# A DeltaNet and Fourier-mixing kernel: unread TensorE products between the steps at the first mixing, and three key pieces moved into the next stage

## The chip, the cores and the metric

The kernel runs on one core of a Trainium2 chip. The metric is the device time of one execution in microseconds (us). All ratios in this document are the mean time of one kernel's fast runs over the mean of the other's fast runs of the same rounds, so they are not quite the ratio of the medians that are quoted. The interval behind a ratio is the 95% interval.

## The reference, cut to what matters

The first half is a delta-rule recurrence over 768 positions for 4 batches and 8 heads of 48 columns; the second half mixes the result with a two-dimensional Fourier transform, normalises it and sends it through a two-layer MLP.

```python
for t in range(S):                       # S = 768, B = 4, H = 8, D = 48
    kt, vt, bt = (k_n[:, :, t], v[:, :, t], beta[:, :, t, None])
    y[:, :, t] = np.einsum('bhd,bhde->bhe', q[:, :, t], state)
    v_old = np.einsum('bhde,bhd->bhe', state, kt)
    state = state + bt[..., None] * np.einsum('bhd,bhe->bhde', kt, vt - v_old)
# ... y becomes x of shape (4, 768, 384)
mixed = np.real(np.fft.fft(np.fft.fft(x, axis=1), axis=2)).astype(np.float32)
u = x + mixed
un = (u - mean(u)) / np.sqrt(var(u) + 1e-06)          # over the 384 columns
return u + np.maximum(un @ w_ch1, 0.0) @ w_ch2        # 384 -> 1536 -> 384
```

## The kernel before

The recurrence is cut into chunks of 64 positions: 12 steps for each batch, 48 in all. A step multiplies a state by prepared keys, subtracts (`U`), multiplies by an inverted triangle (`wt`), and updates the state.

```python
def chain(m):
    b, n = divmod(m, NCH)                                   # NCH = 12 steps for a batch
    # ... 8 products of keys and state into pk
    dve.tensor_tensor(U..., V4[:, c]..., pk, op=ALU.subtract)
    yield
    # ... 8 products of wt and U into pu
    act.activation(U..., pu, ACT.Copy)
    yield
    # ...
    if n < NCH - 1:
        # ... 8 products of keys and U into pS
        dve.tensor_tensor(nst, st, pS, op=ALU.add)          # the state update
    # ...
    yield
```

Keys are prepared for eight steps at a time, in "pieces": two kinds of piece transpose keys through PSUM (`pt`) and copy them (`KQT`); the third multiplies them with themselves (`pg`), and four ScalarE copies put the result into the table `A`. The inversion of the group then starts with a VectorE transpose of `A` into `X`; its result is merged into `Z` and `wt`, which step 16, the first of the third group, needs.

```python
def ps_one(shape, name):                                    # pt, pf, pb, pd, ptr, ph, po
    return ps.tile(shape, F32, tag="one", bufs=2, name=name)
# ...
next_keys = keys(4, 5)                                      # twelve pieces, the third group
key_work = {(7, 0): 2, (8, 2): 3, (9, 0): 1, (10, 2): 2, (11, 0): 1, (11, 1): 2, (11, 2): 1}
first_mixing = fourier(0)
for m in range(1, NCH):
    for i, _ in enumerate(chain(m)):
        # ... other work of the step
        advance(next_keys, key_work.get((m, i), 0))
        # ...
run(rest, *later)
later.clear()
advance(first_mixing)
# ...
def ahead(g):
    if g == 2:
        yield from kept(queries(4, 5))                      # kept: held in program order
    # ...
    yield from invert(g)
    for _ in merge(g):
        yield
```

Step 12 (`n == 0`) is the first of the second batch. In its second part (`i == 1`) the loop issues the whole first mixing at once, with the first MLP products beside it, and only after that does it draw from `pre`, which is `ahead(2)`:

```python
pre, due, started = ahead(2), [0.0, 0.0], False
for m in range(NCH, STEPS):
    b, n = divmod(m, NCH)
    # ...
    for i, _ in enumerate(chain(m)):
        if i < 2:
            advancing(later)
        if n == 0 and i == 1:
            run(*later)
            later.clear()
            if b == 1:
                while advance(first_mixing):
                    if (0, 0) in norms or started:
                        started = advance(channels, 2)      # MLP products
            # ...
        if m > NCH or i > 0:
            due[0] += 4.6 if g == 1 else PRE
            due[1] += SIDE[b]
        while max(due) >= 1.0:
            # ... beside() for due[1]
            if due[0] >= 1.0:
                due[0] -= 1.0
                advance(pre)
```

## Time and profile before

| | before |
|---|---|
| time, median of 3 (range) | 775.79 us (775.71 to 776.6) |
| span of the profiled run, mean clock | 773.7 us, 0.971 |
| TensorE (PE) busy, idle | 679.0 us, 94.7 us |
| VectorE (DVE) busy | 391.7 us |
| MLP products `ph` and `po` | 210.1 and 208.5 us of the PE time |

The engine table, the slices, the stretches of the stage and its chain of waits stand in the prediction below. Two views are added here that the prediction did not use, and that would have mattered. The first is the timeline of TensorE in the kernel before; a line is start, length, engine, source line, operation, output<-inputs, their forms, and the number of records.

```profile
143.28 0.68 PE L131 MATMUL pc<-st,KQT 48*64 48x48 f32 x16
...
167.07 0.45 PE L131 MATMUL pc<-st,KQT 48*64 48x48 f32 x16
...
199.50 0.38 PE L131 MATMUL pt<-pack,qp 128*128 128x128 f32 x2
```

The same 16 records of a step took 0.68 us at 143 us and 0.45 us at 167 us, where the clock is recorded as full. So TensorE ran at a low clock at 143 us too, although the clock record shows 1.00 there: it holds no entry before 144.7 us. It had done so from the start: the 192 records of this product before 144.7 us took 303 ns each in the median, those after 195 us 218 ns. What looks like a first drop of the clock at 148 us is therefore one window at full clock, from 144.7 to 148.1 us, in a low clock that lasts from the start of the kernel to 161.8 us. The mean clock of 0.971 counts the time before 144.7 us as full; counted by the length of the products, this profile has 190.0 us at the low clock. And the first work of `ahead(2)`, the query pieces (`pt` from `qp`), ran at 199.5 us, behind the mixing and not in the idle gap at 152 us.

The second is the timeline of VectorE in the kernel before, same columns; the bracket is an idle time before the instruction and what ended it.

```profile
152.00 1.89 DVE L131 STREAM_TRANSPOSE X<-A 128x1024 f32<-128x1024 f32 x1
...
162.82 0.35 DVE L131 TENSOR_TENSOR st<-st,pc 128x192 f32<-128x192 f32 x1 [2.88 <-PE pc L131]
...
224.03 1.98 DVE L131 STREAM_TRANSPOSE Z<-Y 128x1024 f32<-128x1024 f32 x1
...
238.99 0.35 DVE L131 TENSOR_TENSOR U<-V,pc 128x192 f32<-128x192 f32 x1 [8.20 <-PE pc L131]
```

The third group's inversion begins at 152.00 us as soon as `A` is whole, although the program calls it after the query pieces, and it reaches the merge (`Z`) at 224.03 us. VectorE does much other work in between. The last line is the subtraction of step 16.

### The profile page before, as it was taken

The page shows a single profiled execution, that of the slowest core. Times are in us where ns is not written, and L with a number is a line of the kernel's source. Part 1 is how long each engine was busy: PE and PEld are TensorE (multiplying, and loading weights), DVE is VectorE, ACT ScalarE, POOL GpSimd, SP SyncE. Part 2 cuts the span into 40 slices and gives each one's busy share as a digit, 9 for nine tenths or more (in the row PEclk, how much of TensorE's full clock was granted, in tenths as well). Part 3 has the DMA queues.
Part 4 walks back from the last instruction along what each step waited for, and adds up shares of the span by engine and source line. Part 5 has one row for each costly group of instructions (what it writes and reads, how often), then busy time and mean ns, then how long its engine had stood idle before and what let it go on. Part 6 is the DMA issues. An engine that isn't in the chain of part 4 may idle for free.

```text
span 773.7 us, 18281 instructions
## 1 busy us (share of the span) xinstructions
PE 679.0 (88%) x7768; PEld 487.8 (63%) x7768; DVE 391.7 (51%) x972; ACT 261.4 (34%) x708; POOL 83.3 (11%) x116
## 2 busy tenths in 40 slices
PE   5934598779989989899998999899999989899996
PEld 4622477567647757466756667566667667577683
DVE  2599776877980299336597122989311125300000
ACT  3742355643336512533413535112622022121120
POOL 8010033323100000001100000101000000100000
PEclk9999999877999999999999999899999989999999
DMA  8642032342210221001211110100000000000000
GB/s 182 165 108 50 6 86 63 86 121 68 45 39 18 51 44 32 13 22 38 37 27 25 23 38 7 22 11 22 12 22 2 19 4 1 21 1 21 10 11 20
DMA packets 81041, 30.78 MB, mean 40 GB/s; under 512 B 75856, under 2 KB 77392, under 8 KB 80960
## 3 DMA queue, kind: packets, MB, share of 16 engines
q1 hardware_dynamic: 76560, 21.92, 13.3%
q0 software_dynamic: 2224, 7.31, 2.9%
q8 instruction: 61, 1.00, 0.5%
q10 hardware_dynamic: 2176, 0.39, 0.3%
q14 instruction: 20, 0.16, 0.1%
HBM read 24.87 MB, written 4.72 MB: 38 GB/s over the span
## 4 chain that ended last, share of the span: by engine, by line
PE 54%; DVE 14%; ACT 4%; issue 2%; DMA 1%; SPq 1%; POOL 1%; POOLq 0%; DVEq 0%; ACTq 0%
PE ph L131 20%; PE po L131 18%; DVE X L131 4%; PE pc L131 3%; DVE A L131 3%; PE pf L131 2%; PE pb L131 2%; DVE x L131 2%; ACT wt L131 2%; PE pg L131 2%; PE pt L131 2%; PE py L131 2%; ACT A L131 1%; PE ptr L131 1%; PE pj L131 1%
## 5 line engine op out<-in xcount | busy, mean ns | idle before, releaser
L131 PE MATMUL ph<-unT,w 128*128 128x256 f32 x864 | 210.1, 392 | 4.3 <-ACT hT L131 2.7
L131 PE MATMUL po<-w,hT 128*128 128x384 f32 x576 | 208.5, 504 | 0.1
L131 PEld LDWEIGHTS ph<-unT,w 128*128 128x128 f32 x864 | 159.5, 192 | 31.7 <-ACT hT L131 5.9
L131 PEld LDWEIGHTS po<-w,hT 128*128 128x128 f32 x576 | 105.0, 193 | 63.1 <-issue 3.6
L131 ACT ACTIVATE hT<-ph 128x256 f32<-128x256 f32 x144 | 55.1, 383 | 188.8 <-PE ph L131 188.4
L131 DVE TENSOR_TENSOR x<-x,po 128x384 f32<-128x384 f32 x24 | 13.2, 550 | 108.6 <-PE po L131 108.5
L131 PE MATMUL pg<-KQT 48*64 48x64 f32 (+1 forms) x1152 | 44.9, 295 | 9.5 <-ACT KQT L131 7.2
L131 PEld LDWEIGHTS pg<-KQT 48*64 48x64 f32 x1152 | 34.2, 176 | 25.6 <-ACT KQT L131 14.0
L770 POOL DMA_INDIRECT out_dram<-x,rows_hi x12 | 12.4, 1032 | 332.8 <-DVE x L131 174.1
L131 DVE TENSOR_TENSOR U<-V,pc 128x192 f32<-128x192 f32 x48 | 16.7, 348 | 56.8 <-PE pc L131 56.8
L131 ACT ACTIVATE KQT<-pt 128x256 f32<-128x256 f32 (+1 forms) x84 | 33.2, 414 | 30.8 <-PE pt L131 29.7
L131 DVE TENSOR_TENSOR A<-X 128x30 f32<-128x30 f32 (+14 forms) x120 | 41.3, 344 | 3.0
L131 ACT ACTIVATE U<-pc 128x192 f32<-128x192 f32 x48 | 15.9, 331 | 79.1 <-PE pc L131 75.7
L131 DVE TENSOR_TENSOR X<-X,A 128x30 f32<-128x30 f32 (+14 forms) x120 | 40.7, 339 | 2.8
L131 DVE TENSOR_TENSOR st<-st,pc 128x192 f32<-128x192 f32 x44 | 15.4, 350 | 43.5 <-PE pc L131 36.7
L131 PEld LDWEIGHTS pc<-st,KQT 48*64 48x64 f32 x768 | 19.4, 158 | 26.7 <-DVE st L131 16.5
L131 PE MATMUL pc<-st,KQT 48*64 48x48 f32 x768 | 26.1, 253 | 10.9 <-DVE st L131 10.5
L131 PE MATMUL pt<-pack,qp 128*128 128x128 f32 x96 | 22.5, 331 | 13.9 <-DMA qp<-in_q_dram 13.1
L131 PEld LDWEIGHTS pc<-U,wt 64*64 64x64 f32 x768 | 20.2, 154 | 20.4 <-issue 9.6
L131 PE MATMUL pc<-U,wt 64*64 64x48 f32 x768 | 26.9, 249 | 5.9 <-DVE U L131 4.3
L131 ACT ACTIVATE A<-pj 32x128 f32<-32x128 f32 (+1 forms) x76 | 20.8, 274 | 32.5 <-PE pj L131 31.8
L131 DVE TENSOR_TENSOR x<-x,pb 128x191 f32<-128x191 f32 (+1 forms) x72 | 24.8, 414 | 13.6 <-PE pb L131 13.5
(135 smaller groups left out, 846.5 us busy)
## 6 DMA issues: line engine op xcount, KB each, us to landing
x<-in_moe_w_ch_dram SPq DMA_DIRECT2D x14, 384.0 KB, 3.5
qp<-in_q_dram SPq DMA_DIRECT2D x96, 48.0 KB, 2.4
kp<-in_k_dram SPq DMA_DIRECT2D x80, 48.0 KB, 2.5
V<-in_v_dram SPq DMA_DIRECT2D x56, 48.0 KB, 2.5
w<-in_moe_w_ch_dram POOLq DMA_DIRECT2D x6, 384.0 KB, 7.8
x<-in_moe_w_ch_dram POOLq DMA_DIRECT2D x4, 384.0 KB, 7.9
V<-in_v_dram SPq DMA_DIRECT2D x64, 24.0 KB, 2.1
out_dram<-x SPq DMA_DIRECT2D x8, 192.0 KB, 1.9
```

The costliest lines, as they stand in the source:

```text
L131: ins = getattr(self.engine, name)(*args, **kwargs)
L770: nc.gpsimd.indirect_dma_start(out=out.rearrange("b s m -> (b s) m"), out_offset=bass.IndirectOffsetOnAxis(ap=rows_hi[:, i:i + 1], axis=0) ...
```

## The change

Its intent is to keep the TensorE clock up at the first mixing, where TensorE has gaps. A constant table is multiplied with itself into a buffer that nobody reads, up to three times in each of steps 11 to 14. Beside that, three of the twelve key pieces of the third group leave step 11 and become the first work of `ahead(2)` (two others are issued one place later than before).

```diff
+    def busy(m):
+        if NCH - 1 <= m < NCH + 3:
+            mm(ps_one([128, 384], "idle"), stab[:, 0:128], stab[:, 0:384], True)
 ...
     def chain(m):
 ...
         dve.tensor_tensor(U.rearrange(ue, e=2), V4[:, c].rearrange(ue, e=2), pk, op=ALU.subtract)
+        busy(m)
         yield
 ...
         act.activation(U.rearrange(ue, e=2), pu, ACT.Copy)
+        busy(m)
         yield
 ...
             dve.tensor_tensor(nst, st, pS, op=ALU.add)
+            busy(m)
 ...
-    key_work = {(7, 0): 2, (8, 2): 3, (9, 0): 1, (10, 2): 2, (11, 0): 1, (11, 1): 2, (11, 2): 1}
+    key_work = {(7, 0): 2, (8, 2): 3, (9, 0): 1, (10, 2): 1, (11, 0): 1, (11, 2): 1}
 ...
         if g == 2:
-            yield from kept(queries(4, 5))
+            yield from kept(seq(next_keys, queries(4, 5)))
```

## The prediction

> **What bounds the kernel now.** I read the engine table first, then the slices, then the stage that the diff touches: steps 11 to 14 of the recurrent chain and the first mixing, 143 to 195 us.
>
> ```profile
> PE 679.0 (88%) x7768; PEld 487.8 (63%) x7768; DVE 391.7 (51%) x972; ACT 261.4 (34%) x708; POOL 83.3 (11%) x116
> ...
> PE   5934598779989989899998999899999989899996
> ...
> DVE  2599776877980299336597122989311125300000
> ...
> PEclk9999999877999999999999999899999989999999
> ```
>
> Over the whole span TensorE (PE) is the fullest engine, and after 230 us it is busy 510 of 544 us. The clock row shows a dip in slices 8 to 10 (19.3 us each), and there VectorE (DVE) is as full as PE. So this is a stage of two coupled engines, followed by one bound by PE. The next view gives busy time in stretches of 3.41 us; columns are stretch, length, busy us (instructions) of PE, its weight loads, DVE, ACT, POOL, then the clock.
>
> ```profile
> 144.70:148.11 3.41, 1.40 (x44) 0.97 (x36) 3.41 (x9) 2.69 (x8) 0.65 (x2) 1.00 0.30 68
> 148.11:151.53 3.42, 2.42 (x92) 2.42 (x94) 1.83 (x6) 2.82 (x9) 1.33 (x2) 0.50 0.19 30
> 151.53:154.94 3.41, 1.52 (x32) 0.81 (x31) 3.41 (x5) 0.73 (x2) 0.33 (x1) 0.50 0.24 40
> 154.94:158.35 3.41, 2.27 (x28) 2.10 (x23) 3.41 (x13) 0.00 (x0) 0.46 (x1) 0.50 0.21 36
> 158.35:161.77 3.42, 3.42 (x29) 3.10 (x29) 1.59 (x8) 1.00 (x3) 0.83 (x1) 0.50 0.80 262
> 161.77:165.18 3.41, 3.41 (x45) 3.06 (x43) 1.78 (x4) 3.41 (x9) 0.58 (x1) 1.00 0.22 52
> 165.18:168.59 3.41, 2.80 (x59) 2.06 (x57) 3.21 (x10) 1.91 (x5) 1.35 (x2) 1.00 0.69 224
> 168.59:172.01 3.42, 0.45 (x16) 0.32 (x16) 2.99 (x12) 2.20 (x5) 0.80 (x2) 1.00 0.34 107
> 172.01:175.42 3.41, 2.74 (x23) 2.19 (x24) 2.83 (x8) 0.98 (x2) 1.69 (x2) 0.50 0.00 0
> 175.42:178.83 3.41, 3.41 (x10) 2.45 (x10) 3.31 (x6) 0.00 (x0) 3.08 (x2) 0.50 0.51 143
> 178.83:182.25 3.42, 3.42 (x25) 2.41 (x24) 3.01 (x11) 1.15 (x3) 0.59 (x2) 0.50 0.38 121
> 182.25:185.66 3.41, 3.41 (x24) 2.74 (x24) 3.03 (x9) 1.58 (x5) 1.45 (x2) 1.00 0.00 0
> ```
>
> The clock is half in four stretches from 148.1 (13.7 us) and three from 172.0 (10.2 us), each time after a stretch with little PE work (1.40 and 0.45 us). Elsewhere stretches with 1.98 us (223.2) and 1.81 us (284.7) kept the full clock, one with 1.86 us (329.0) lost it. So I put the limit near 1.8 us of 3.41. Which waits follow? In the chain of waits a line is start, length, work:
>
> ```profile
> 172.52 0.49 DVE un L131
> 173.14 1.51 PE ptr L131 x6
> ...
> 175.05 3.15 PE pb L131 x8
> 178.20 2.86 PE ph L131 x6
> ...
> 191.74 0.79 PE pd L131 x4
> ...
> 192.55 1.21 DVE x L131 x4
> ```
>
> From 173.1 to 192.5 the chain that ends last lies on PE without a break, its first 9.1 us at half clock. Then it goes over to DVE (the inversion of the third group), whose result is merged at 233 us and lets step 16 run. The totals of waits from 140 to 235 us add: DVE for PE 3.2 us at the state update, 2.0 and 1.4 us at the mixing's additions; PE for ACT 2.6 us at the key products `pg`; DVE for ACT 2.0 us.
>
> **What the Trainium skill says.** "TensorE: Matmul & The Clock Gate", section "What's actually happening": the clock is either half or full, decided over a free-running window of about 3.4 us. The trace agrees: every change lies on a grid of 3.41 us, which is why I cut the view so. Its section "Why this matters for your kernels" asks for no idle gap above about 3 us; here PE had been idle 1.6 us (146.5 to 148.1) when the clock fell, so this trace goes by the busy share of the window. "FP8 and Floating Point Precision", section "TensorE Precision Notes", gives true FP32 four passes; an estimate for 384 columns at 2.4 GHz is 4 x 384 / 2.4 = 640 ns. The trace has two records for each such product: 24 records of `po` (128x384) took 8.01 us, 334 ns each, 667 ns a product. It agrees.
>
> **The change, part by part.**
> 1. Dummy products. Step 11 calls it twice (its state update, with the third call, is skipped as the last step of a batch), steps 12 to 14 three times: 11 products, 22 records, 11 x 0.667 = 7.3 us of PE at full clock, 14.7 us at half. They read only the table, so they wait for no data, but each takes one of two PSUM buffers shared with `pf`, `pb`, `pt`, `ph`, `po`.
> 2. Where they lie. PE's idle gaps in the stage are 146.5 to 149.1, 152.8 to 154.7, 155.5 to 156.7, 168.0 to 171.0 and several of about 0.6 us up to 173.1, some 10 us. By their place in the program, the two of step 11, the first of step 12 and two or three of step 13 fall beside these: about 6, free. The other 5 fall into full stretches: 3.3 us of added work, of which I put 2.6 us (the last of step 13, three of step 14) on the chain above.
> 3. What they buy. Window 144.7: 1.40 + 2 x 0.667 = 2.7 us, over the limit, so the first drop should go. In window 151.5 the work at full clock is about 0.8, a dummy makes 1.5, and the three displaced key pieces (two pairs of transposes at about 0.4, one `pg` at 0.7) make 3.0, so it should hold. The mixing's `pf` then runs at full speed: PE is busy about 5.0 us from 156.7 to 161.7, so up to 2.5 us less, and DVE's 2.9 us wait at 159.9 shrinks by as much. Window 168.6 has 0.45, plus one or two dummies: 1.1 to 1.8 us, at the limit. If it holds, 9.1 us at half clock become 4.6, up to 4.5 us less on the chain; even if it fails, step 14's dummies make the next windows denser and may end the slow part a window early (about 1.7 us).
> 4. Key pieces. Three of twelve (two transposes with copies, one `pg` with four ACT copies, 2.1 us of ACT) leave step 11, where ACT is the queue that PE (2.6 us) and DVE (1.6 us of the 2.0) wait for, and go where ACT idles 7.8 us (152.5 to 160.3). Worth about 1 us. Against it, the 1.9 us transpose that starts the inversion comes later; it stood ahead of step 12's state copy, so DVE only swaps the two.
>
> Sum: first drop -2.5, second drop half of -4.5 = -2.2, key pieces -1, dummies on the path +2.6, gives -3.1 us. DVE allows it: it is idle 13 us between 140 and 230, 6.6 of it the three waits for PE above. The dense PE stage after 233 us hands any earlier end of the merge through to the end nearly whole. I add -0.9 us because the later windows of the stage get a shorter wait on `pb` and `pd` (3.4 us), which I have only counted in part.
>
> **Rivals.** *The clock stays low anyway*: window 168.6 remains below the limit, or a displaced dip appears. For it: 1.1 us is a likely value there. Then about -2 to +1: 774 to 777. *The dummies become the wait*: they need a buffer that DVE empties only after six additions (2.1 us), and [...]a dummy stuck for a buffer holds real products. For it: both buffers are in use in the mixing; against it, the real products there wait for the same buffers. Up to +3: 777 to 779. *DVE is the bound*: it is busy 8.9 us of 10 from 170 to 180, so faster PE only makes PE wait; the gain halves, 773 to 774. *Everything holds*: full clock from 144.7 on, -7 us or a little more: 767 to 769.
>
> **Range and chances.** The predicted time is 775.79 - 4.0 = 771.8 us. The good rival and the bad one give 765.5 to 777.5 us. Faster by 2% means under 760.3 us, 15.5 us less, more than the 13 us that DVE idles in the stage: 0.02. Slower by 2% needs twice the whole 7.3 us of dummies: 0.01. Within 2%: 0.97.
>
> **What would show it.** In the changed kernel the clock at 148 to 162 us should read 1.00, and at 172 to 182 us shorter or gone; 22 records of `idle` of about 0.33 us spacing; the wait at the state update (2.9 us) below 1 us; `pd` ending 2 to 5 us before 192.5; step 16's first products 3 to 5 us before 238. The prediction is wrong if the clock dips remain in number and length, if `idle` shows waits for DVE or ACT above 1 us each, or if the gain at 230 us is lost again to a clock drop later on.

## The result and the profile after

The changed kernel took 783.67 us in the median of 4 runs (783.06 to 787.03), the kernel before 776.19 us (775.71 to 776.72, 4 runs): a ratio of 1.0105 (1.0075 to 1.0135). Run again later with five rounds the ratio was 1.0077 (1.0041 to 1.0113). It is within 2%, as most of the chances said, but it is slower by 6 to 8 us and lies outside the range of 765.5 to 777.5 us.

The engine table and three of the rows of 40 slices (19.5 us each) of the kernel after:

```profile
PE 689.3 (88%) x7790; PEld 489.8 (63%) x7790; DVE 391.6 (50%) x972; ACT 260.5 (33%) x708; POOL 84.1 (11%) x116
...
PE   5934588979987999899998999899999989899996
...
DVE  2599776856785169746597111988411125300000
...
PEclk9999999989999999999999999899999999999999
```

TensorE has 22 more records, the 11 unread products, and is busy 10.3 us more. Its idle time fell by only 2.6 us (94.7 to 781.4 - 689.3 = 92.1 us); the difference is the 7.7 us of the longer span. VectorE does the same work (391.6 us), but is less full in the slices 9 to 11, counted from 1 (5, 6, 7 tenths; before 7, 7, 9), and does more of it later. The clock row dips less, but the record of this kernel begins only at 155.8 us, and the products before that are as slow as in the kernel before (`pc` from `st`: 303 ns). Counted from the start the low clock lasts 190.9 us here and 190.0 us before.

The next view is the stretches of 3.41 us of the kernel after, with the prediction's columns (stretch, length, busy us of PE, its weight loads, DVE, ACT, POOL, the clock, and two DMA columns).

```profile
155.79:159.20 3.41, 3.41 (x57) 3.15 (x57) 2.83 (x11) 0.79 (x2) 1.52 (x1) 1.00 0.35 62
159.20:162.62 3.42, 3.42 (x44) 2.96 (x42) 0.35 (x1) 2.27 (x7) 0.10 (x1) 1.00 0.92 317
...
166.03:169.44 3.41, 0.79 (x40) 0.54 (x32) 3.39 (x12) 1.09 (x3) 0.58 (x2) 1.00 0.60 205
169.44:172.86 3.42, 2.29 (x17) 1.77 (x17) 2.51 (x7) 1.91 (x5) 2.03 (x3) 0.50 0.02 5
...
179.68:183.10 3.42, 3.42 (x18) 3.03 (x17) 2.44 (x8) 2.83 (x8) 1.79 (x3) 1.00 0.20 31
```

In this profile the low clock ends at 155.79 us instead of 161.77 us, so the mixing's first products run at full clock. The second dip stays, from 169.44 to 179.68 us (10.2 us, as before), after a stretch with 0.79 us of TensorE work. Where were the unread products that should have filled it? They are `idle` in the timeline of TensorE of the kernel after:

```profile
143.97 1.65 PE L131 MATMUL idle<-stab 128*128 128x384 f32 x2
...
152.53 3.35 PE L131 MATMUL idle<-stab 128*128 128x384 f32 x4
...
196.48 0.38 PE L131 MATMUL pt<-pack,kp 128*128 128x128 f32 x2
...
198.73 0.81 PE L131 MATMUL idle<-stab 128*128 128x384 f32 x2
```

Two records are one product. Four products ran by 155.9 us (a line at 147.38 us is left out), at 1.65 us each where a product at full clock takes 0.81 us; none ran between 155.9 and 198.7 us; the other seven came from 198.7 to 217.9 us, where TensorE is full anyway. The moved key pieces (`pt` from `kp`, then `pg`) came at 196.5 us.

VectorE's timeline after shows what those pieces hold up:

```profile
160.13 0.35 DVE L131 TENSOR_TENSOR st<-st,pc 128x192 f32<-128x192 f32 x1 [1.51 <-PE pc L131]
...
200.08 1.97 DVE L131 STREAM_TRANSPOSE X<-A 128x1024 f32<-128x1024 f32 x1 [7.99 <-ACT A L131]
...
238.11 2.03 DVE L131 STREAM_TRANSPOSE Z<-Y 128x1024 f32<-128x1024 f32 x1
```

The state update waits 1.51 instead of 2.88 us: the gain that was looked for. It did not come a second time. In a later profile of the same kernel (h1 below) the low clock lasted to 163.8 us, the first block of the mixing (`pf`, 14 records) took 2.94 us as before, not 1.62 us, and the same update waited longer than before:

```profile
163.09 0.35 DVE L131 TENSOR_TENSOR st<-st,pc 128x192 f32<-128x192 f32 x1 [4.75 <-PE pc L131]
```

So two profiles of one kernel disagree on whether the early products shorten the low clock. Over all 18 profiles it is not shown that they do: from 140 to 165 us the nine with early products have 10.9 to 23.8 us of low clock, the nine without 15.9 to 24.1 us. In the first profile, the inversion starts at 200.08 instead of 152.00 us, after 7.99 us in which VectorE stood idle until `A` was whole, and `Z` is made 14.1 us later. From 160 to 200 us VectorE idled some 19 us, before 9 us. The subtraction of step 16 moved from 238.99 to 250.98 us. The chain of waits of the kernel after tells it in one piece:

```profile
189.97 6.67 PE ph L131 x30
...
197.22 0.37 PE pt L131 x2
197.83 0.74 PE pg L131 x29
198.59 0.67 ACT A L131 x2
...
200.08 1.98 DVE X L131
```

Five groups of MLP products (`ph`), then the key pieces, then ScalarE's copies to `A`, then the inversion. Where are the 7.7 us lost? Every kernel leaves 1440 records of MLP products (`ph` and `po`) on TensorE, so the end of the n-th of them tells how far the work that must be done has come. The 48th ended 3.0 us earlier than before, the 96th 2.6 us later (218.5 us before), the 144th 1.7 us later (237.3), the 288th 5.9 us later (303.9), the last 7.7 us later. So 5.6 us go between records 48 and 96, where the late key pieces, the query pieces and the seven late unread products stand, and 4.2 us between records 144 and 288, which follow the late merge: TensorE is idle 7.0 us there, before 3.4 us. Neither stretch holds any low clock, in either kernel.

### The profile page after: what moved, and what is told of

Same layout as the page of the kernel before. It is cut to its first block, busy times and chain, and to the rows that moved or that the text cites.

```text
span 781.4 us, 18327 instructions
## 1 busy us (share of the span) xinstructions
PE 689.3 (88%) x7790; PEld 489.8 (63%) x7790; DVE 391.6 (50%) x972; ACT 260.5 (33%) x708; POOL 84.1 (11%) x116
## 3 DMA queue, kind: packets, MB, share of 16 engines
q1 hardware_dynamic: 76560, 21.92, 13.7%
## 4 chain that ended last, share of the span: by engine, by line
PE 59%; DVE 23%; ACT 8%; DMA 3%; issue 3%; SPq 2%; POOL 1%; POOLq 0%; ACTq 0%; DVEq 0%
PE ph L131 19%; PE po L131 18%; DVE A L131 5%; PE pc L131 5%; DVE X L131 5%; PE pg L131 3%; DVE w L131 3%; ACT wt L131 3%; PE pj L131 3%; PE pt L131 2%; ACT A L131 2%; PE pf L131 2%; DVE x L131 2%; PE pb L131 2%; PE py L131 2%
## 5 line engine op out<-in xcount | busy, mean ns | idle before, releaser
L131 PE MATMUL po<-w,hT 128*128 128x384 f32 x576 | 212.2, 511 | 0.1
L131 PEld LDWEIGHTS po<-w,hT 128*128 128x128 f32 x576 | 106.9, 195 | 66.0 <-issue 7.3
L779 POOL DMA_INDIRECT out_dram<-x,rows_hi x12 | 12.4, 1033 | 314.8 <-DVE x L131 147.5
L131 ACT ACTIVATE U<-pc 128x192 f32<-128x192 f32 x48 | 15.9, 331 | 82.0 <-PE pc L131 64.2
L131 PE MATMUL pt<-pack,qp 128*128 128x128 f32 x96 | 22.4, 331 | 13.7 <-DMA qp<-in_q_dram 13.2
```

Source lines behind the costliest of these rows:

```text
L131: ins = getattr(self.engine, name)(*args, **kwargs)
L779: nc.gpsimd.indirect_dma_start(out=out.rearrange("b s m -> (b s) m"), out_offset=bass.IndirectOffsetOnAxis(ap=rows_hi[:, i:i + 1], axis=0) ...
```

## The experiments

**Theory.** Two things cost time: the key pieces, because the loop issues `ahead(2)` behind the whole mixing, which starts the inversion 48 us late; and the unread products as plain TensorE work, the seven late ones above all. **The products rival**: the cost is the unread products alone, through the shared buffers or their time, and the pieces are harmless. **The clock rival**: the remaining dip and other dips of the clock set the time. The expectations quoted below have letters of their own, and there theory A is the key pieces alone and rival B the products alone.

Sixteen kernels ran in four calls, on the chips numbered 6, 11, 0 and 6; each call had its own runs of the kernel before: medians 774.63, 776.97, 776.62 and 775.87 us. All outputs were correct. "+2.9 us" below is (ratio - 1) x 776.

### Each part alone

**e1_dummies_only** is the change without its last two hunks.

```diff
-    key_work = {(7, 0): 2, (8, 2): 3, (9, 0): 1, (10, 2): 1, (11, 0): 1, (11, 2): 1}
+    key_work = {(7, 0): 2, (8, 2): 3, (9, 0): 1, (10, 2): 2, (11, 0): 1, (11, 1): 2, (11, 2): 1}
-            yield from kept(seq(next_keys, queries(4, 5)))
+            yield from kept(queries(4, 5))
```

> The dummy products of the change, the key pieces left where they were before. Theory A (the displaced key pieces cost the time: they are issued behind the whole first mixing, so the third group's inversion starts 48 us late): the inversion's first transpose is back near 152 us, step 16 near 238 us, and the time is 770 to 776 us. Rival B (the 11 dummy products cost the time, 7.3 us of TensorE at full clock): 781 to 784 us, as with the whole change.

Measured: 776.97 us (775.82 to 777.44), ratio 1.0023 (1.0005 to 1.004): +1.8 us. The inversion starts at 152.42 us and `Z` at 223.48 us, as before; step 16 is 1.9 us later. Dips still fall at 156.5 us (6.8 us) and 170.2 us (13.7 us). The time missed the range of theory A by 1 us; it is 4 us below that of rival B. The products alone do not explain 6 to 8 us.

**e2_keys_only** is the kernel before with only the last two hunks.

```diff
-    key_work = {..., (10, 2): 2, (11, 0): 1, (11, 1): 2, (11, 2): 1}
+    key_work = {..., (10, 2): 1, (11, 0): 1, (11, 2): 1}
-            yield from kept(queries(4, 5))
+            yield from kept(seq(next_keys, queries(4, 5)))
```

> The key pieces moved as in the change, no dummy product. Theory A: the inversion's first transpose stays near 200 us, and the time is 782 to 788 us, both clock dips staying. Rival B: 774 to 778 us, as before the change.

Measured: 777.97 us (777.51 to 778.35), ratio 1.0037 (1.002 to 1.0054): +2.9 us. VectorE's timeline of this kernel shows the late inversion without any unread product:

```profile
199.20 1.94 DVE L131 STREAM_TRANSPOSE X<-A 128x1024 f32<-128x1024 f32 x1 [7.67 <-ACT A L131]
```

So the pieces are not harmless (the products rival falls), and their place in the loop is the cause of the late start. The time itself fell into the range of rival B, 4 us below that of theory A: the late start is as theory A has it, its price is not. Step 17 is 9.0 us later and the kernel only 2.9 us slower: most of the delay is regained, because TensorE does MLP products meanwhile. Part of the price comes by way of the clock: this trace has a low stretch of 13.7 us from 239.9 us, behind the late merge, where the kernel before runs at full clock.

### Where the key pieces are issued

**e3_keys_after_11** is the change with the three pieces issued after step 11, ahead of the mixing.

```diff
     run(rest, *later)
     later.clear()
+    run(next_keys)
     advance(first_mixing)
 ...
-            yield from kept(seq(next_keys, queries(4, 5)))
+            yield from kept(queries(4, 5))
```

> The whole change, but the three displaced key pieces are issued right after step 11 and ahead of the first mixing, so at most about 5 us later than before. Theory A (their place behind the mixing is what costs, not that they left step 11): within 4 us of the kernel with dummies alone, so 768 to 777 us. Rival C (fewer pieces in step 11 is bad by itself, or the dummies need them as company): 780 us or more.

Measured: 782.96 us (780.51 to 787.51), ratio 1.0123 (1.0089 to 1.0157). A miss: `X` from `A` started at 157.61 us and `Z` stood at 224.02 us, as the theory wanted, yet the kernel was as slow as the change. Step 16 came 5.2 us late all the same. Two lines of this kernel's timelines show by what, of TensorE and then of VectorE:

```profile
218.80 0.81 PE L131 MATMUL idle<-stab 128*128 128x384 f32 x2
...
236.27 0.96 DVE L131 TENSOR_TENSOR V<-V,ln 128x768 f32<-128x768 f32 x1 [4.50 <-DMA V<-in_v_dram]
```

The first is one of four unread products that stand between the MLP products (`po`) and the products of the recurrence (`pc`) from 215.6 to 221.3 us. The scaling of the next values (`V`), which step 16 reads, waited 4.50 us for its transfer; before, it waited 0.68 us and came at 218.90 us. So an early inversion did not help where all eleven products stand on TensorE. The next three kernels take this one apart.

**h3_keys_after_11_bare** is the same placing in the kernel before, with no unread product.

```diff
-    key_work = {..., (10, 2): 2, (11, 0): 1, (11, 1): 2, (11, 2): 1}
+    key_work = {..., (10, 2): 1, (11, 0): 1, (11, 2): 1}
 ...
     later.clear()
+    run(next_keys)
     advance(first_mixing)
```

> Only the key pieces, issued between step 11 and the first mixing; no dummy products. Theory A2 (the cost of the key move is the inversion that starts 48 us late because the pieces are issued behind the mixing): inversion near 157 us, and within 1.5 us of before, 774 to 778 us. Rival G (any move of the pieces pushes steps 12 to 15 behind the mixing, as step 14 was 20 us late in the same kernel with dummies): 779 to 783 us with the inversion on time.

Measured: 773.98 us (772.67 to 774.57), ratio 0.9953 (0.993 to 0.9977): -3.6 us. VectorE's timeline of this kernel:

```profile
154.55 1.93 DVE L131 STREAM_TRANSPOSE X<-A 128x1024 f32<-128x1024 f32 x1
...
238.33 0.35 DVE L131 TENSOR_TENSOR U<-V,pc 128x192 f32<-128x192 f32 x1 [7.28 <-PE pc L131]
```

The inversion starts 2.6 us later than before and step 16 still runs 0.7 us earlier; here `V` is scaled after `Z` and nothing waits for its transfer. Moving the pieces out of step 11 was a good idea; moving them behind the mixing was not. Rival G falls: step 14 came 19.1 us later here too, and the kernel was faster. Why it gains 3.6 us and not the 0.7 us of step 16 was not traced to a line; its profile ends only 1.1 us before that of the kernel before. It was run at another time. All six runs had a mean clock of 0.982.

**k2_keys_after_11_late_dummies** adds to h3 the six products of steps 13 and 14.

```diff
+        if NCH < m < NCH + 3:
+            mm(ps_one([128, 384], "idle"), stab[:, 0:128], stab[:, 0:384], True)
```

> Key pieces between step 11 and the mixing (alone that ran 3.6 us below before), with the six dummies of steps 13 and 14 only, which run after 198 us. If the late dummies are what made the same kernel with all eleven 9 us slower than before: 779 us or more. If they cost at most their own time: 774 to 778 us.

Measured: 775.80 us (775.13 to 782.0), ratio 0.9996 (0.9958 to 1.0035): 3.3 us more than h3's ratio. Six products at full clock are 6 x 0.65 = 3.9 us.

**k3_keys_after_11_early_dummies** adds to h3 the four early products of steps 11 and 12 instead: `NCH - 1 <= m < NCH + 1`, without the third call in the step.

> The same with the two dummies of step 11 and the first two of step 12 only, 1.65 us each at half clock, ahead of step 12 and the mixing. If the early ones are the cost, because they hold TensorE back from step 12 at half clock: 779 us or more. If not: 773 to 777 us.

Measured: 776.53 us (772.09 to 781.4), ratio 1.0001 (0.9955 to 1.0047): 3.7 us more than h3's.

**k4_keys_after_11_again** is e3 once more, with five rounds.

> The kernel with all eleven dummies and the key pieces ahead of the mixing, once more, as the mark for the two above on the same chip: 779 to 784 us.

Measured: 781.87 us (777.58 to 787.12), ratio 1.0076 (1.0025 to 1.0127). The six runs form two groups, three at 777.6 to 778.2 us with mean clocks of 0.977 to 0.980 and three at 785.5 to 787.1 us with 0.967 to 0.971. With the bare kernel at -3.6 us, the early and the late products cost about as much each, 3 to 4 us, and both together 9.5 us (k4) to 13 us (e3): at least the sum. These differences are taken across different chips, and the intervals are 2 to 4 us wide on each side, so only their sign and rough size are shown. The profiles say where they fall: between MLP records 48 and 96 k2 takes 3.8 us more than h3, close to the 3.9 us of its six late products, and the 48th record of k3 comes 2.2 us later than that of h3.

### Which unread products

**e5_dummies_11_12** is e1 with five products, those of steps 11 and 12.

```diff
-        if NCH - 1 <= m < NCH + 3:
+        if NCH - 1 <= m < NCH + 1:
```

> Dummy products in steps 11 and 12 only (5 of 11), key pieces as before. Theory A: the first clock dip is gone as with all eleven, and six dummies that ran among other full work after 198 us are away, each 0.667 us: 3 to 4 us below the kernel with all dummies if that stretch is bound by TensorE, the same within 1 us if it is bound by VectorE's inversion.

Measured: 775.13 us (773.05 to 777.5), ratio 1.0004 (0.9974 to 1.0033), step 16 at -0.14 us. No gain and no cost that is resolved; against e1 the ratio is 1.5 us lower, which lies between the two forecasts and decides for neither.

**f1_change_early_dummies** makes the same edit in the full change.

> The whole change (key pieces moved too), but without the six dummy products of steps 13 and 14, all of which ran after 198 us in the changed kernel, in stretches full of other products. Theory D (TensorE's stream of products from 195 to 245 us sets the end, and these six stand in it): 6 x 0.65 = 3.9 us below the changed kernel, so about 779 to 780.5 us. Rival E (the late inversion of the third group, 14 us later than before, is what sets the end, and the dummies only fill time that TensorE would wait): within 1 us of the changed kernel, 783 us.

Measured: 781.08 us (778.24 to 784.31), ratio 1.006 (1.0014 to 1.0106): +4.7 us. The change stood at +8.1 and +6.0 us, so D and E are not told apart.

**f2_late_dummies** is the kernel before with the six products of steps 13 and 14 alone (`NCH < m < NCH + 3`).

> The kernel before with the six dummy products of steps 13 and 14 alone: the disputed cost by itself. Theory D: part of their 3.9 us lies in TensorE's wait for the inversion at 224 to 231 us (2.7 us), so 1.5 to 4 us above before. Rival E: within 0.7 us of before.

Measured: 774.44 us (773.74 to 777.76), ratio 0.9993 (0.9957 to 1.0029), step 16 at -0.35 us. Alone, in the kernel before, they show no cost. In the profile they cost 3.4 us between MLP records 48 and 96, and 2.9 us of it come back by record 144, where TensorE's idle time falls from 2.7 us to nothing: they filled the wait for the inversion.

**h2_keys_late_dummies** is the change with these six products alone.

> Key pieces moved, only the six dummies of steps 13 and 14 (all run after 198 us), none in steps 11 and 12. The kernel with the key move alone was 3 us above before; the whole change 8. If the late dummies are what the sum of the parts lacks: 781 to 784 us. If it is the early dummies, or their meeting with the key move: 777 to 779 us.

Measured: 779.87 us (775.84 to 782.04), ratio 1.0026 (0.9994 to 1.0058): +2.0 us, no more than the pieces alone.

**h1_change_again** is the change itself, five rounds.

> The whole change once more, as the mark for the others of this call. Expected 781 to 786 us (before it read 783.7)[...].

Measured: 784.49 us (778.18 to 785.91), ratio 1.0077 (1.0041 to 1.0113): +6.0 us. The two parts alone add up to 2.9 + 1.8 = 4.7 us. The rest, 1.3 us against this run and 3.5 us against the first measurement, could not be given to the early or the late products: f1 and h2 lie within each other's intervals. It stays open.

What the profiles add is where each kernel loses its time. The table gives the end of MLP records against the profile of the kernel before, in us; plus is later. It rests on one profile of each.

| | at record 48 | 48 to 96 | 96 to 144 | 144 to 288 | rest | end |
|---|---|---|---|---|---|---|
| the change | -3.0 | +5.6 | -0.9 | +4.2 | +1.8 | +7.7 |
| h1, the change again | -2.3 | +5.6 | -0.7 | +4.2 | +2.0 | +8.8 |
| e1, products only | +0.8 | +3.3 | -2.2 | 0.0 | -0.2 | +1.6 |
| e2, pieces only | -3.9 | +1.2 | -2.8 | +8.3 | 0.0 | +3.0 |
| h3, pieces ahead of the mixing | -1.4 | +1.0 | -0.3 | 0.0 | -0.4 | -1.1 |

The column from 144 to 288 separates the kernels. All five with the pieces behind the mixing (the change, h1, e2, f1, h2) lose 4.2 to 8.3 us there; the other twelve take the 66.6 us of the kernel before, to 0.1 us. The two with 8.2 and 8.3 us (f1, e2) are those with a low clock of 13.7 us in it. All eight kernels with the late products lose 3.3 to 5.6 us from 48 to 96, the nine others at most 1.9 us. Each part alone regains 2 to 3 us before record 144; both together regain 0.7 to 0.9 us.

### Does the clock at the mixing matter at all?

**f4_early_and_mixing** leaves the keys as before, keeps four products in steps 11 and 12, and puts four more inside the mixing, where the second dip starts.

```diff
             mm(pb[:, HD + 1:DM], F[0:HD - 129, 1, 1, ts], dtab[0:HD - 129, 1, HD + 1:DM], False)
+            if b == 0 and T == 0:
+                for _ in range(4):
+                    mm(ps_one([128, 384], "idle"), stab[:, 0:128], stab[:, 0:384], True)
```

> What the change aimed at, with the dummies where the second dip starts: key pieces as before, two dummies in step 11, two in step 12, and four inside the first mixing behind its first block of products, where TensorE waits 3 us for VectorE. If the dips cost what I estimated and the dummies lie in waits: no half clock between 158 and 300 us, step 14's input 3 to 5 us earlier, the time 770 to 773 us. Rival F (VectorE is the bound of this stage, so TensorE's speed does not matter): no dips, but 774 to 777 us.

Measured: 777.15 us (774.81 to 778.4), ratio 1.0004 (0.9972 to 1.0035). By the record, the low clock in the stage shrank from 13.7 + 10.2 us to 3.4 + 6.8 us; the record begins 2.8 us later here, at 147.5 us, so that 10.8 us less are left from 140 to 200 us. The forecast of no half clock up to 300 us failed also at 226.0 us, where 3.4 us of low clock are new. Two stretches of this kernel, then two lines of VectorE's timeline, the last of them step 16's subtraction:

```profile
171.41:174.83 3.42, 2.24 (x63) 1.70 (x63) 2.08 (x8) 1.09 (x3) 1.27 (x2) 1.00 0.00 0
174.83:178.24 3.41, 3.41 (x18) 2.55 (x18) 2.26 (x9) 0.98 (x2) 2.45 (x3) 0.50 0.23 33
```

```profile
218.36 0.96 DVE L131 TENSOR_TENSOR V<-V,ln 128x768 f32<-128x768 f32 x1 [1.57 <-DMA V<-in_v_dram]
...
238.99 0.35 DVE L131 TENSOR_TENSOR U<-V,pc 128x192 f32<-128x192 f32 x1 [7.38 <-PE pc L131]
```

The clock fell after a stretch with 2.24 us of work in 63 small products, which is above the limit of 1.8 us that the prediction had read. And step 16 stands at 238.99 us, exactly where it stood before. What became of the 10.8 us less of low clock? VectorE's inversion was 1.1 us ahead of before at 216.5 us (the instruction `A<-X` on 130 columns came at 216.50 instead of 217.59 us). Then VectorE waited 1.57 us for the transfer of `V` (before 0.68 us), so `Z` was 0.2 us ahead. Behind it TensorE ran eight `po` and thirty `ph` records between the merge's products and step 16, the `po` at the new low clock (4.07 instead of 2.85 us), and the rest was gone. Part of the gain went into the longer wait for a transfer, and the last 0.2 us were gone behind that new dip; why only 1.1 us of it had reached VectorE by 216 us is not shown.

**f5_mixing_only** keeps only the four products in the mixing.

> Key pieces as before, only the four dummies inside the first mixing. The first dip stays, the second (10 us at half clock from 172 us) should be gone. Estimate: 9 us of products at half clock become 4.5, of which VectorE lets half through: 772 to 774.5 us. Rival F: 774 to 776 us.

Measured: 773.52 us (773.14 to 778.54, 5 runs), ratio 0.9964 (0.9936 to 0.9991): -2.8 us. Step 16 is at +0.47 us, so the gain is not made there. The second dip shrank to 6.8 us and did not go. The profiled run is its slowest, so its trace does not show where the gain is made.

**h4_every_mixing** adds three products ahead of the first `pf` of each later mixing.

```diff
+            if b > 0 and a == 0:
+                for _ in range(3):
+                    mm(ps_one([128, 384], "idle"), stab[:, 0:128], stab[:, 0:384], True)
             for i in range(2):
                 rows = min(128, w - 128 * i)
```

> A try for a better version: key pieces as before, four dummies inside the first mixing behind its first block of products, and three ahead of the first product of each of the other three mixings, where TensorE waits 1.5 to 3.2 us for VectorE and the clock fell at 332 and 633 us. If those dips cost half their length (3.4 + 6.8 us, so 5 us): 768 to 772 us. If the dummies only shift the dips: 773 to 777 us.

Measured: 773.27 us (770.91 to 775.81), ratio 0.995 (0.9924 to 0.9977): -3.9 us. It is faster than before; against f5 the difference is not resolved. The two late dips that it aimed at (332.4 and 632.8 us in the kernel before) are gone, those at 315.7 and 493.2 us are not, and one at 390.8 us is new. The gain of the profile is made at the last mixing: the 864th MLP record (580.5 us before) ends 0.4 us later than before, the 1080th (670.1 us) 2.4 us earlier, and so does the last. So the change's idea seems to hold there, where the dip fell on the products of the mixing and on MLP products after VectorE's inversions are done; it rests on one profile, and on that of k1 below.

**k1_keys_after_11_and_mixing** joins the two versions that beat both kernels, h3 and h4.

> A try for the best version: key pieces between step 11 and the mixing, and the dummies only in the mixings (four behind the first block of the first, three ahead of each later one). Each part alone was 3.6 and 3.9 us below before. If they add: 768 to 771 us. If both remove the same wait: 772 to 775 us.

Measured: 774.42 us (773.25 to 778.29), ratio 0.9978 (0.9943 to 1.0013). The gains do not add. Its profile too gains 2.8 us between records 864 and 1080, where the dip at 632.8 us is gone. The best versions are h3 and h4, each about 0.5% faster than the kernel before.

On the clock rival: within one kernel the times follow the clock in part. Eleven runs of the kernel before in the last call go from 774.3 us at a mean clock of 0.984 to 780.35 us at 0.971, but a run at 0.969 took 775.87 us, so it also matters where a dip falls. This scatter of some 3 us either way widens every interval here. It does not make the change slow in its first profile: counted from the start, the low clock lasts 190.9 us there and 190.0 us before, and the span is 7.7 us longer. (The mean clocks, 0.978 and 0.971, count the time before the record begins as full.) In h1 the low clock lasts 198.8 us, so part of its time may be the clock's.

## Why the prediction was wrong, step by step

- **Where they lie (part 2) failed.** The prediction took steps 11 to 14 of the program for the same stretch of time as the mixing. It expected six products in gaps, free, and five in full stretches. The loop issues the whole mixing in the middle of step 12, so four ran before it and seven behind it, at 198.7 to 217.9 us. None could fill the stretch at 166 us.
- **Their cost (part 1) was mis-sized.** The count of 11 products and 22 records was right, and 0.667 us at full clock too (0.65 us from start to start in a stream of products, 0.81 to 0.91 us alone). But the four early ones ran at the low clock: 6.65 us instead of 4 x 0.667 = 2.7 us. TensorE was busy 10.3 us more in all; the prediction had 2.6 us of added work on the path.
- **Key pieces (part 4) failed, with the sign.** They were to land in ScalarE's idle time at 152.5 to 160.3 us for -1 us. As the first work of `ahead(2)` they ran at 196.5 us: +2.9 us alone (e2). "DVE only swaps the two" was wrong: the inversion's first transpose needs `A` and was 48 us late, and TensorE lost 4.2 us between MLP records 144 and 288 for it. The idea as such was right: with the pieces still ahead of the mixing (h3) the move was worth -3.6 us.
- **What they buy (part 3) failed.** The prediction took the clock row at its word ("a dip in slices 8 to 10"); the products were at the low clock from the start, and in the kernel after the early unread products were too, so the sum 1.40 + 2 x 0.667 us for the first window does not hold. In the first profile the low clock ended 6 us earlier and the wait at the state update fell to 1.51 us (the prediction asked for below 1 us), but in the second profile of the same kernel (h1) neither happened: that was luck of the run, as far as two profiles tell. The limit near 1.8 us did not even fit the lines it was read from, where 1.81 us kept the clock and 1.86 us lost it. The second dip stayed, as the first rival had named, though not for its reason: no product was there at all. The -2.5 and -2.2 us were not there to be had at step 16: in f4, with 10.8 us less of low clock, step 16 did not move. That speaks for the third rival, VectorE as the bound, with two things added: the transfer of `V`, for which VectorE waited 1.57 us there and which no part of the prediction had, and a new dip at 226.0 us, which the prediction's first rival had named.
- **"Hands any earlier end of the merge through nearly whole" failed.** In e2 step 17 came 9.0 us later and the kernel took 2.9 us more. In h3 step 16 came 0.7 us earlier and the kernel took 3.6 us less. TensorE fills the time before step 16 with MLP products that have to be done anyway, so the time of step 16 is a poor measure of the end.
- **The second rival was not seen.** TensorE's idle time before all `idle` products adds to 1.7 us in the whole trace, so the shared buffers did not stall the products.
- **What held.** The two coupled engines and the chain over TensorE in the stage were read correctly, and so was the class "within 2%", though with the sign against the forecast. The view meant to catch the error did so: step 16's products were to come 3 to 5 us earlier and came 12 us later.

## What to carry to other kernels

Before you move work, find in the trace where the work that now stands beside its new place really runs: one line, the query pieces at 199.5 us, would have shown that `ahead(2)` begins behind the mixing. Ask next who waits for the moved work; three short pieces held up an inversion that took 38 us even when VectorE had little else to do (200.08 to 238.11 us after). Products that only keep the clock up are real work on TensorE, and here they took twice as long where they were issued at the low clock (1.65 against 0.81 us); count them as added time unless the trace shows a wait that they fill (f2), or work of the engine that sets the end that they speed up (the last mixing in h4). And look at the profile of a second execution before you call a change of the clock the work of an edit.

## What the Trainium skill lacked or had wrong

- **When the clock falls.** "TensorE: Matmul & The Clock Gate", section "Why this matters for your kernels", asks for no idle gap above about 3 us. That does not tell when the clock falls here: it fell after stretches of 3.41 us with 1.40, 0.45 and 0.79 us of work, and in f4 even with 2.24 us in 63 small products, and held with 1.81 us elsewhere. Its section "A second HAM failure mode: psum-queue depth-cycling" does tell of short idle times between groups of products that make the clock go up and down, but with no measure of them. Busy time alone does not give a limit here, and no page has one.
- **When it comes back.** The same page, section "What's actually happening", has the clock full after one busy window or more. In the kernel before it came back after one full stretch (158.35 to 161.77 us), and at 182.25 us only after two (175.42 to 182.25 us). The page's words allow both; it does not say what decides.
- **How much runs differ by it.** That section calls the window free-running and run-variable and the warm-up penalty under 1% of a typical span. The traces agree that it varies: the first full clock came at 155.8 and at 163.8 us in two profiles of the change. But it came late, at 144.7 to 164.1 us in all 18 traces, a fifth of the span. And the runs of k4 differ by 9.5 us (1.2%), in two groups with mean clocks of 0.977 to 0.980 and 0.967 to 0.971; which dips make the difference is not shown.
- **A clock record that begins late.** The page's section "Seeing it yourself" warns that the clock's events can be unreliable. Here there is no entry before 144.7 us (before) or 155.8 us (after), and the view shows 1.00 there while products ran slowly: 0.68 against 0.45 us for the same 16 records, and 1.65 against 0.81 us for an unread product. That section sets the spacing of products beside the clock's events in its example, but it advises to check the events against a total of throttled time, not against the length of products of one form.
